# Two-stage kernel of linear attention and a noisy top-2 mixture of experts: key decay ahead of the routing work, weight loads and splits in other steps, a third buffer for x rows, row gathers one by one

## The chip, the cores and the metric

The kernel runs on one core of a Trainium2 chip. The metric is device time in microseconds (us), the median of three runs. Engines are called PE (TensorE matmul), PEld (its weight loads), DVE (VectorE), ACT (ScalarE), POOL (GpSimd) and SP (SyncE, which here only issues DMAs). An engine carries out its instructions in the order of the program, and so does each of the two queues that issue DMAs: SP's (plain copies) and POOL's (gathers and scatters by row index).

## The reference, cut to what matters

Linear attention with decay, over 4 batches, 8 heads, 768 positions and 64 channels, in blocks:

```
intra = (qb @ kb^T * Dmask) @ vb
inter = (qb * lam_pow) @ kv_state
out   = intra + inter
kv_state = lam_block * kv_state + (kb * rev_pow)^T @ vb
```

Its output, seen as x of 3072 tokens by 512 channels, goes into a mixture of 8 experts:

```
noisy = x @ w_gate + log1p(exp(x @ w_noise)) * noise
top2, weights = two largest of noisy, softmax over the two
out[token] += weight * (relu(x[token] @ w1[e]) @ w2[e])     # for both experts e of the token
```

`kb * rev_pow` is what this text calls the **key decay**, and `(kb * rev_pow)^T @ vb` the **state products**.

## The kernel before, in words

**Attention.** The 3072 tokens are 24 chunks of 128; a unit u is two chunks, so there are 12 units. A loop over steps t = 0 to 11 (L885) prepares unit u = t + 1 and finishes unit t. A step issues, in this order: the transposes of the keys (`trans_k`, L297) and of the queries (`trans_q`, L310); the loads of k, q and v of unit t + 3 on SP's queue (L161, L157); the state products (`kv`, L385) and the state update on DVE (`state`, L394 to L398); a portion of routing work (`advance(FILLS)`, L896); the second half of the attention of unit t (`intra`, `inter`, L350) and its copy to SBUF (`evac_o`); the transposes back to token rows (`store_x`, L413: each of a unit's two chunks goes by ACT into a tile `xc`, L414 and L415, and by SP's queue to the rows `x_tok` in DRAM, L417); the gate's products (`products`, L404); the scores of the next unit (`scores`, L338, masked on DVE at L341); and the gate logits (`logits`, L429).

Only then comes `kdecay(t + 2)` (L919): two POOL multiplications (L326) that write the decayed keys of unit t + 2 into the tile `kd`. There is one buffer of `kd`, so they wait for the state products of unit t + 1, and the state products of unit t + 2, in the next step, wait for them. The load of k of unit t + 4 takes the buffer of the keys that `kdecay(t + 2)` reads.

Behind `kdecay` stand, in the same step: the first two row gathers of expert 0, once, in the first step after its lists are there (L920); a weight split, in the steps that the table `SPLITS` names (L927; ACT makes the high part at L747, DVE the low part at L748); a second portion of routing work, `advance(FILL - SPLIT)` in a step with a split and `advance(FILL)` in one without; and a load of 512 KB of weights on SP's queue, in the steps that `LOADS` names (L936). The weights are staged in four `wst` buffers; a load waits for the split of the fourth load before it.

**Routing in portions.** The gate of a group of chunks (`gate`, `weights`, `places`, `build`) is a list of Python generators. `advance(n)` issues their instructions until their costs, as the program puts them (0.21 for most), add up to n. The constants are FILLS = 3.4, FILL = 2.0 and SPLIT = 1.2. Most of it runs on DVE; `weights` (L484 to L500) is issued in one go and is a chain of some 24 small POOL instructions, which begins when the two largest logits are found on DVE (`mx`, L468). The routing of group 0 (chunks 0 to 7) enters the list in step 4, that of group 1 in step 8, that of group 2 after the loop.

**Experts.** Expert 0 takes its tokens in three parts of 2, 2 and 3 tiles of 128 rows (`parts(0)`, the loop at L987), so that it can begin while later tokens are still being routed. Each part is a first matmul over eight blocks f of 128 hidden columns (`gemm1`, L801; ACT and DVE evacuate each block at L807 and L811 into `ht`) and a second one tile by tile (`gemm2`, L839). In the second part, at tile 2, `lists_done` (L970) completes the row lists; it gathers tiles 4 to 6 of expert 0, frees the four `wst` buffers with small POOL copies (L978), and gathers tiles 0 to 3 of expert 1. Ahead of the third part the loop gathers tiles 4 to 6 of expert 1 (L988 to L990). Behind the third part's eight blocks the outputs of tiles 0 to 3 of expert 0 are scattered (L1018 to L1020), and those of tiles 4 to 6 behind their own `gemm2`. From block 4 on, the third part also issues the loads of expert 1's first weights (L1015) and the transposes of expert 1's rows (L1017). A gather or a scatter (L770, L823, L858) moves 128 rows of 2 KB.

Experts 1 to 7 (L1106) do the same in two parts each. There a gather stands behind a one-element POOL copy out of the `ht` block just evacuated (L1121), so that one gather follows each block.

The tile `xc` has the two buffers of its pool, of 2 KB per partition each.

Of the kernel before, what the change touches and what calls it, by code (L numbers as in the profile page):

```python
# [31 lines left out]
C = 128  # L32
# [29 lines left out]
OPUS = 0.21  # L62
FILL, SPLIT, FILLS = 2.0, 1.2, 3.4
FILL1, FILLG = 0.9, 4.6
LOADS = {0: (1, 0), 1: (1, 1), 2: (1, 2), 3: (1, 3), 4: (2, 0), 5: (2, 1), 9: (2, 2), 10: (2, 3)}
SPLITS = {2: (1, 0), 3: (1, 1), 4: (1, 2), 5: (1, 3), 6: (2, 0), 7: (2, 1)}
X1 = ((), (0,), (1,), (2,), (3,), (4,), (5, 6))
WARM = (14, 4, 4)
GB = (0, 8, 16, NCH)
# [52 lines left out]
def kernel(  # L122
# [143 lines left out]
    def advance(n):  # L266
        while n > 0 and jobs:
            j = next(jobs[0], "end")
            if j == "end":
                jobs.pop(0)  # L270
            elif j == "step":
                break
            else:
                n -= j or OPUS
# [114 lines left out]
    def state(u):  # L389

        for a, p in enumerate(KV[u]):
            sn = SA[u + a, 1 - a] = next(states)
            if (u, a) not in SA:
                nc.vector.tensor_copy(sn, p[:, :, :D])  # L394
                continue
            for hp in range(HP):
                nc.vector.scalar_tensor_tensor(sn[:, hp, :], SA[u, a][:, hp, :], QS[:, hp, C - 1:C], p[:, hp, :D],
                                               op0=MULT, op1=ADD)  # L398
# [9 lines left out]
    def store_x(u):  # L408

        for a in range(2):  # L410
            p = bank()
            for d in range(DB):
                nc.tensor.transpose(p[:, d, :], XO[u][:, a, d, :], identf)  # L413
            xc = aw.tile([128, DB, C], FT, name="xc")  # L414
            nc.scalar.activation(xc, p, AF.Copy)  # L415
            g = 2 * u + a
            nc.sync.dma_start(x_tok[g * C:(g + 1) * C, :DM], xc.rearrange("p d i -> p (d i)"))  # L417
# [467 lines left out]
    for t in range(NST):  # L885
        u = t + 1
        if u < NST:
            trans_k(u)
        load(t + 3, "kt")
        if u < NST:  # L890
            trans_q(u)
        load(t + 3, "qt")
        if u < NST:
            kv(u)
            state(u)
            advance(FILLS)  # L896
        else:
            store_x(t - 1)
            products(t - 1)
            for j in range(PARTS0[0]):  # L900
                trans_rows(0, j)
            logits(t - 1)
            advance(FILLS)
        intra(t)
        load(t + 3, "vt")
        inter(t, 0)
        evac_o(t)
        if u < NST:
            if t:
                store_x(t - 1)  # L910
                products(t - 1)
            scores(u)
            inter(u, 1)
            if t:
                logits(t - 1)
        if 2 * t in GB[1:]:
            b = GB.index(2 * t) - 1
            jobs.extend((routing(b), build(early(b))))
        kdecay(t + 2)  # L919
        if REC and not got:  # L920
            for j in range(PARTS0[0]):
                gather_rows(0, j, GB[1] * C)
            got.append(t)
        if built and u < NST:
            enlist(built, False)
            built.clear()
        if t in SPLITS:  # L927
            split_w(SPLITS[t][0], 0, SPLITS[t][1])
        advance(FILL - (SPLIT if t in SPLITS else 0))
        if "w" in RT.get(0, {}):  # L930
            store_w(0)
        if RT.get(0, {}).get("listed") == GM and not REC:
            assert "w" not in RT[0]
            read_lists(0, PARTS0[0])
            load_rec(0)
        if t in LOADS:  # L936
            load_w(LOADS[t][0], 0, LOADS[t][1])
        if t >= NST - 2:
            zero_out(3)
        if t == 2:  # L940
            nc.sync.dma_start(nz, sub(noise, 0, [[E, 128], [128 * E, NCH], [1, E]]))
# [28 lines left out]
    def lists_done():  # L970
        enlist(units[2])
        read_lists(sum(PARTS0[:2]), NTL)
        which_expert(1, nc.sync)
        load_rec(1)
        for j in range(4, 7):
            gather_rows(0, j)
        for _, _, _, buf in units[2]:
            nc.gpsimd.tensor_copy(spacer, buf[0:1, 0:2].bitcast(FT))  # L978
        for j in range(4):
            gather_rows(1, j)  # L980


# [2 lines left out]
        return lambda: [trans_rows(0, t) for t in ts]  # L985

    for i, (t0, n) in enumerate(parts(0)):  # L987
        if i == 2:  # L988
            for t in range(t0, t0 + n):
                gather_rows(1, t)  # L990
        for f in range(FB):
            if i or f >= 2:
                gemm1(0, t0, n, f)
            if i == 0:
                if f == 0:
                    split_w(2, 0, 2)
                elif f < 3:
                    split_w(2, 0, 3, f - 1)
                while f == 3 and len(built) < len(units[1]):
                    advance(0.01)  # L1000
                if 2 <= f < 7:
                    nc.scalar.activation(XG[f], zero, AF.Copy)
                zero_out(2)
                if f == FB - 1:
                    enlist(units[1])
                    read_lists(PARTS0[0], PARTS0[0] + PARTS0[1])
                    for t in range(PARTS0[0], PARTS0[0] + PARTS0[1]):
                        gather_rows(0, t, GB[2] * C)
            if i == 1:
                zero_out(1)  # L1010
                advance(FILL1)
                if "w" in RT[2]:
                    store_w(2)
            if i == 2 and f >= 4:
                load_w(1, 1, f - 4)  # L1015
                for j in X1[f - 4]:
                    trans_rows(1, j)  # L1017
        if i == 2:  # L1018
            for t in range(t0):
                scatter_out(0, t, PV[t])  # L1020
        if i == 0:
            for c in range(0, GB[3] - GB[2], 2):
                units[2].append((2, c, 2, wp.tile([128, F], FT, name="wst", bufs=4).bitcast(BF)))
            advance(FILLG)
        if i == 1:
            finish(2)
            advance(50)
            assert not jobs and "w" not in RT[2]
        then = {1: {12: rows(2, 3)}, 2: {1: lists_done}, 3: {16: rows(4, 5, 6)}}
        for t in range(t0, t0 + n):  # L1030
            gemm2(0, t, then.get(t, {}))
            if t == 0:
                finish(2, "gated")
            if t == 1:
                advance(FILLG)
            if i == 2:
                scatter_out(0, t, PV[t][:size(0, t), :])
            if i == 2:
                for j in range((0, 2, 3)[t - t0], (2, 3, 4)[t - t0]):
                    split_w(1, 1, j)  # L1040
                    load_w(2, 1, j)
                for j in X1[t]:
                    trans_rows(1, j)
# [174 lines left out]
```

## Time and profile before

| | us |
|---|---|
| median of 3 runs | 746.75 |
| the three runs | 745.95, 746.75, 749.08 |
| the profiled execution, its own time | 749.22 |
| its span, first to last instruction | 747.3 |
| PE busy in the span | 722.4 (97%) |
| DVE, ACT, POOL busy | 349.9, 222.6, 237.5 |
| mean granted TensorE clock | 0.988 of full speed |

The profile is one execution; its own time is 1.9 us above its span. The clock column is the share of full speed (2.4 GHz) that the TensorE clock was granted in a stretch: 1.00 is 2.4 GHz and 0.50 is 1.2 GHz. "Idle before" in a timeline row is the time in which that engine did nothing before the row's instruction, with what ended it; "issue" there means that nothing in the profile was waited for. The share of the DMA engines is a mean over 16 of them and can come out a little above 1.

### The profile page before, as it was taken

The numbers are of one execution on the slowest core, as the hardware profiler recorded it, in microseconds if no ns is written. First come the engines' busy times: TensorE is split into PE (matmuls) and PEld (weight loads), VectorE is DVE, ScalarE is ACT, GpSimd is POOL, SyncE is SP. The second block draws the span as 40 slices with busy tenths as digits, with TensorE's granted clock in tenths as the row PEclk, the third lists the DMA queues.
The fourth block names the chain that finished last, engine by engine and source line by source line (L and its number), as shares of the span: only waits on it lengthen the run. The fifth ranks groups of instructions, "written<-read, shape, count | busy, mean of one in ns | idle before, by whom it ended". The sixth has DMA issues, their size and how long they took to land. (4 is left out here: it accounts for less than half of the span.)

```text
span 747.3 us, 15521 instructions
## 1 busy us (share of the span) xinstructions
PE 722.4 (97%) x6170; PEld 618.6 (83%) x6170; DVE 349.9 (47%) x890; ACT 222.6 (30%) x381; POOL 237.5 (32%) x384
## 2 busy tenths in 40 slices
PE   6999989999989999999999999999999999999995
PEld 4888778889878898888888888888888898889884
DVE  5555869769236544443434334434432452335210
ACT  0456544442033321232123212321232242214100
POOL 2311243313613443423441344235222423121311
PEclk9899999999999999999999999999999999999998
DMA  7799955571734634352435153526442543230211
GB/s 183 200 293 239 301 149 168 199 285 30 186 107 143 193 99 156 121 156 58 157 117 155 57 158 116 158 54 178 129 128 72 179 151 104 80 111 25 66 42 38
DMA packets 92052, 103.48 MB, mean 138 GB/s; under 512 B 38582, under 2 KB 64710, under 8 KB 91976
## 3 DMA queue, kind: packets, MB, share of 16 engines
q1 hardware_dynamic: 80408, 66.08, 31.4%
q0 software_dynamic: 11568, 36.37, 15.3%
q8 instruction: 50, 0.82, 0.4%
q14 instruction: 26, 0.21, 0.1%
HBM read 77.93 MB, written 25.74 MB: 139 GB/s over the span
## 5 line engine op out<-in xcount | busy, mean ns | idle before, releaser
L801 PE MATMUL pS<-xth,w1h 128*128 128x512 f32 (+3 forms) x544 | 182.4, 335 | 2.0 <-issue 1.2
L801 PE MATMUL pS<-xth,w1l 128*128 128x512 f32 (+3 forms) x544 | 181.1, 333 | 0.8 <-issue 0.7
L801 PE MATMUL pS<-xtl,w1h 128*128 128x512 f32 (+3 forms) x544 | 181.1, 333 | 0.4 <-issue 0.4
L811 DVE SCALAR_TENSOR_TENSOR ht<-pS,ht 128x256 fp32r<-128x256 f32 (+3 forms) x176 | 76.4, 455 | 136.0 <-ACT ht L807 127.3
L839 PE MATMUL pO<-w2h,ht 128*128 128x512 f32 x384 | 124.4, 395 | 0.0
L839 PE MATMUL pKV<-w2h,ht 128*128 128x512 f32 x384 | 124.3, 394 | 0.0
L807 ACT ACTIVATE ht<-pS 128x512 fp32r<-128x512 f32 (+3 forms) x136 | 65.5, 484 | 188.3 <-PE pS L801 175.2
L858 POOL DMA_INDIRECT out_dram<-ot,rec x46 | 60.0, 1305 | 172.6 <-DVE ot L851 161.9
L801 PEld LDWEIGHTS pS<-xth,w1h 128*128 128x128 f32 x544 | 103.3, 190 | 11.0 <-issue 1.3
L801 PEld LDWEIGHTS pS<-xth,w1l 128*128 128x128 f32 x544 | 103.3, 190 | 10.1 <-issue 1.3
L801 PEld LDWEIGHTS pS<-xtl,w1h 128*128 128x128 f32 x544 | 103.4, 190 | 9.8 <-issue 1.1
L782 ACT ACTIVATE xth<-pS 128x512 fp32r<-128x512 f32 (+2 forms) x53 | 29.8, 573 | 196.7 <-PE pS L780 186.6
L839 PEld LDWEIGHTS pO<-w2h,ht 128*128 128x128 f32 x384 | 72.1, 188 | 14.8
L839 PEld LDWEIGHTS pKV<-w2h,ht 128*128 128x128 f32 x384 | 72.1, 188 | 14.7
L839 PE MATMUL pO<-w2l,ht 128*128 128x512 f32 x192 | 74.9, 390 | 0.0
L839 PE MATMUL pKV<-w2l,ht 128*128 128x512 f32 x192 | 74.9, 390 | 0.0
L770 POOL DMA_INDIRECT xg<-x_tok,rec x46 | 49.8, 1083 | 30.5 <-issue 25.5
L823 POOL DMA_INDIRECT pv<-out_dram,rec x46 | 47.2, 1026 | 29.1 <-issue 26.0
L851 DVE SCALAR_TENSOR_TENSOR ot<-pO,wr,pv 128x512 f32<-128x512 f32 x21 | 15.8, 751 | 79.1 <-PE pO L839 79.1
L851 DVE SCALAR_TENSOR_TENSOR ot<-pKV,wr,pv 128x512 f32<-128x512 f32 x21 | 15.8, 751 | 77.6 <-PE pKV L839 77.6
L326 POOL TENSOR_TENSOR kd<-kt,Mk 128x512 f32<-128x512 f32 x24 | 24.9, 1056 | 72.0 <-PE pR L385 36.2
L748 DVE TENSOR_TENSOR w2l<-wst,w2h 128x1024 fp32r<-128x1024 f32 (+1 forms) x33 | 39.2, 1191 | 11.3 <-ACT w2h L747 11.3
(220 smaller groups left out, 956.9 us busy)
## 6 DMA issues: line engine op xcount, KB each, us to landing
wst<-in_moe_w_dram SPq DMA_DIRECT2D x48, 512.0 KB
wst<-in_moe_w_dram SPq DMA_DIRECT2D x32, 256.0 KB
kt<-in_k_dram SPq DMA_DIRECT2D x12, 512.0 KB
qt<-in_q_dram SPq DMA_DIRECT2D x24, 256.0 KB
vt<-in_v_dram SPq DMA_DIRECT2D x12, 512.0 KB
x_tok<-xc SPq DMA_DIRECT2D x24, 256.0 KB
out_dram<-zero SPq DMA_DIRECT2D x24, 256.0 KB
xg<-x_tok,rec POOLq DMA_INDIRECT x46
```

The lines of the kernel that those rows point to most:

```text
L326: nc.gpsimd.tensor_mul(kd[:, :, s], kt[:, :, s], mask(s, slice(0, HP), slice(C - 1, C)).to_broadcast([128, HP, 2, D]))
L748: nc.vector.tensor_tensor(lo[:, r], st[:, r], hi[:, r].bitcast(FT), op=SUB)
L770: nc.gpsimd.indirect_dma_start(out=XG[t][:size(e, t)], out_offset=None, in_=x_tok[:rows, :], in_offset=bass.IndirectOffsetOnAxis(ap=REC[e, ...
L782: nc.scalar.activation(hi, p, AF.Copy)
L801: nc.tensor.matmul(p, W1[a][d][:, fs], xt(b, cs)[:, d], start=(d == 0 and i == 0), stop=(d == DB - 1 and i == 2))
L807: nc.scalar.activation(ht(e, 0, f, cs), p, AF.Relu)
L811: nc.vector.scalar_tensor_tensor(ht(e, 1, f, c), p[:, r], 0.0, ht(e, 0, f, c).bitcast(FT), op0=OP.max, op1=SUB)
L823: nc.gpsimd.indirect_dma_start(out=PV[t][:size(e, t), :], out_offset=None, in_=out, in_offset=bass.IndirectOffsetOnAxis(ap=REC[e, t], axis=0),
L839: nc.tensor.matmul(p, ht(e, a, f, cs), W2[b][f // 2][:, f % 2, :], start=(i == 0), stop=(i == len(terms) - 1))
L851: nc.vector.scalar_tensor_tensor(o, p, w, pv, op0=MULT, op1=ADD)
L858: st = nc.gpsimd.indirect_dma_start(out=out, out_offset=bass.IndirectOffsetOnAxis(ap=REC[e, t], axis=0), in_=o, in_offset=None, bounds_che ...
```

## The change

Five edits. (1) `kdecay(t + 2)` and the one-time gathers of expert 0 are issued right behind `state(u)`, ahead of the portion of routing work, for steps 0 to 10. (2) The loads of weights move from steps 0, 1, 2, 3, 4, 5, 9, 10 to 0, 1, 4, 5, 7, 8, 9, 10 and their splits from 2 to 7 to 2, 3, 6, 7, 9, 10; with the splits, the larger second portion of routing work moves to steps 4 and 5 and the smaller one to steps 9 and 10. (3) `xc` has three buffers. (4) `lists_done` gathers tiles 0 and 1 of expert 1 instead of 0 to 3; in the third part of expert 0, behind each block f, a one-element POOL copy reads the block and then, for f = 0 to 4, tile f + 2 of expert 1 is gathered. (5) For f = 5 to 7 tile f - 5 of expert 0 is scattered instead; tile 3 follows behind the blocks.

```diff
-LOADS = {0: (1, 0), 1: (1, 1), 2: (1, 2), 3: (1, 3), 4: (2, 0), 5: (2, 1), 9: (2, 2), 10: (2, 3)}
-SPLITS = {2: (1, 0), 3: (1, 1), 4: (1, 2), 5: (1, 3), 6: (2, 0), 7: (2, 1)}
+LOADS = {0: (1, 0), 1: (1, 1), 4: (1, 2), 5: (1, 3), 7: (2, 0), 8: (2, 1), 9: (2, 2), 10: (2, 3)}
+SPLITS = {2: (1, 0), 3: (1, 1), 6: (1, 2), 7: (1, 3), 9: (2, 0), 10: (2, 1)}
...
-            xc = aw.tile([128, DB, C], FT, name="xc")
+            xc = aw.tile([128, DB, C], FT, name="xc", bufs=3)
...
             kv(u)
             state(u)
+            kdecay(t + 2)
+            if REC and not got:
+                for j in range(PARTS0[0]):
+                    gather_rows(0, j, GB[1] * C)
+                got.append(t)
             advance(FILLS)
...
-        kdecay(t + 2)
-        if REC and not got:
-            for j in range(PARTS0[0]):
-                gather_rows(0, j, GB[1] * C)
-            got.append(t)
...
-        for j in range(4):
+        for j in range(2):
             gather_rows(1, j)
...
-        if i == 2:
-            for t in range(t0, t0 + n):
-                gather_rows(1, t)
         for f in range(FB):
             if i or f >= 2:
                 gemm1(0, t0, n, f)
+            if i == 2:
+                nc.gpsimd.tensor_copy(spacer, ht(0, 0, f, columns(0, t0, n))[0:1, 0:1].bitcast(FT))
+                if f < 5:
+                    gather_rows(1, f + 2)
+                else:
+                    scatter_out(0, f - 5, PV[f - 5])
...
         if i == 2:
-            for t in range(t0):
+            for t in range(FB - 5, t0):
                 scatter_out(0, t, PV[t])
```

## Rows read from the trace of the kernel before

**Rows 1.** The page's head and its part 1, the whole span.
```profile
span 747.3 us, 15521 instructions
PE 722.4 (97%) x6170; PEld 618.6 (83%) x6170; DVE 349.9 (47%) x890; ACT 222.6 (30%) x381; POOL 237.5 (32%) x384
```

**Rows 2.** Waits of PE: engine, line, releaser, total us, times, longest us.
```profile
PE pS L385 <- POOL kd L326: 4.8, 4, 2.0
PE pS L338 <- issue: 2.7, 3, 1.6
PE pS L801 <- issue: 2.3, 4, 0.9
```

**Rows 3.** Windows: length, busy of PE, PEld, DVE, ACT, POOL, PEclk, DMA share, GB/s.
```profile
50.79:60.78 9.99, 9.99 (x258) 8.90 (x258) 6.29 (x16) 6.20 (x11) 2.06 (x2) 1.00 0.83 212
60.78:72.04 11.26, 10.41 (x235) 9.08 (x234) 6.26 (x13) 6.25 (x11) 2.06 (x2) 1.00 1.08 292
72.04:82.31 10.27, 10.13 (x259) 8.95 (x258) 8.37 (x31) 6.03 (x11) 2.06 (x2) 1.00 1.01 287
82.31:94.48 12.17, 11.22 (x273) 9.36 (x273) 11.39 (x51) 6.25 (x11) 3.50 (x16) 1.00 1.00 297
94.48:108.81 14.33, 12.18 (x242) 10.72 (x239) 8.93 (x28) 6.03 (x11) 8.41 (x14) 0.88 0.59 159
...
119.38:130.27 10.89, 10.49 (x261) 9.15 (x257) 9.91 (x43) 5.25 (x10) 4.34 (x4) 1.00 0.29 86
130.27:141.16 10.89, 10.89 (x249) 9.27 (x249) 7.94 (x39) 5.15 (x10) 4.83 (x21) 1.00 0.34 122
...
200.07:220.34 20.27, 17.85 (x110) 16.67 (x108) 5.98 (x19) 4.20 (x10) 7.37 (x12) 0.92 0.58 174
...
240.00:738.00 498.00, 498.00 (x2559) 423.61 (x2558) 194.48 (x362) 130.12 (x207) 162.80 (x231) 1.00 0.39 115
```

**Rows 4.** Timeline of PE, steps 6 and 7: start, us, instruction, idle before.
```profile
92.57 0.56 PE L338 MATMUL pS<-qT,kT 64*64 64x128 f32 x12 [0.95 <-issue]
...
98.33 0.33 PE L385 MATMUL pS<-vt,kd 64*64 64x64 f32 x2 [1.47 <-POOL kd L326]
...
99.34 0.86 PE L385 MATMUL pS<-vt,kd 64*64 64x64 f32 x22 [0.68 <-POOL kd L326]
```

**Rows 5.** Timeline of POOL, steps 6 and 7.
```profile
89.71 0.20 POOL L492 TENSOR_TENSOR wa<-mx 128x8 f32<-128x8 f32 x1 [11.95 <-DVE mx L468]
...
97.23 2.06 POOL L326 TENSOR_TENSOR kd<-kt,Mk 128x512 f32<-128x512 f32 x2
```

**Rows 6.** A window of step 7, columns as in rows 3.
```profile
102.00:104.00 2.00, 2.00 (x39) 1.71 (x33) 1.93 (x10) 0.00 (x0) 1.36 (x4) 0.50 1.24 307
```

**Rows 7.** Timeline of ACT, step 4.
```profile
69.46 0.60 ACT L415 ACTIVATE xc<-pS 128x512 f32<-128x512 f32 x1 [0.87 <-DMA x_tok<-xc]
```

**Rows 8.** Groups by line, 20 to 170 us: busy us, mean ns, idle before.
```profile
L748 DVE TENSOR_TENSOR w1l<-wst,w1h 128x1024 fp32r<-128x1024 f32 x4 | 4.9, 1214 | 0.0
```

**Rows 9.** Timeline of DVE, step 10.
```profile
139.08 2.48 DVE L341 TENSOR_TENSOR at<-pS,Mk 128x512 f32<-128x512 f32 x4 [2.88 <-PE pS L338]
```

**Rows 10.** Timeline of POOL, 189 to 228 us: first, last and next of the burst.
```profile
189.61 1.11 POOL L770 DMA_INDIRECT xg<-x_tok,recs  x1 [8.17 <-DVE recs L611]
...
208.12 0.98 POOL L858 DMA_INDIRECT out_dram<-pv,recs  x1 [0.47 <-issue]
...
227.14 1.71 POOL L858 DMA_INDIRECT out_dram<-pv,recs  x1 [17.95 <-DVE pv L854]
```

**Rows 11.** Timeline of SP's queue: expert 1's first weights.
```profile
193.51 4.43 SPq L733 DMA_DIRECT2D wst<-in_moe_w_dram  x6
```

**Rows 12.** Timeline of PE in the third part of expert 0: first and last of four.
```profile
207.76 0.39 PE L801 MATMUL pS<-xth,w1l 128*128 128x320 f32 x1 [0.74 <-issue]
...
210.61 0.62 PE L801 MATMUL pS<-xth,w1h 128*128 128x320 f32 x1 [0.86 <-issue]
```

**Rows 13.** Timeline of ACT in the same part, the first block's evacuation.
```profile
206.37 0.44 ACT L807 ACTIVATE ht<-pS 128x320 fp32r<-128x320 f32 x1 [7.60 <-PE pS L801]
```

## The prediction, made before the changed kernel ran

> **What bounds the kernel now.** I read the page's head first: PE is busy for 722.4 of 747.3 us, no other engine for half of the span [rows 1]. The kernel is a chain of PE work, and what a change can win is PE's idle time, about 25 us, and stretches in which PE works at less than full clock. So the second view is PE's list of waits [rows 2]: three entries are large, 4.8 us for the key decay on POOL, and 2.7 and 2.3 us called "issue", where nothing visible was waited for. The third view is windows cut at the step boundaries (each begins with a step's first key transposes) and at the stages of expert 0 [rows 3]. An undisturbed step takes 9.99 us, without a gap. Step 4 (60.78 to 72.04) takes 11.26, step 6 (82.31) 12.17, step 7 (94.48) 14.33. The third part of expert 0 (200.07 to 220.34) has PE idle for 20.27 - 17.85 = 2.42 us at a mean clock of 0.92. From 240 to 738 PE is never idle: nothing to win there, and a microsecond won earlier reaches the end whole. Only those four places bear on this change.
>
> **Key decay.** In step 7 PE waits 1.47 and 0.68 us for the decayed keys [rows 4], 2.15 together, which is all its idle time there (14.33 - 12.18) [rows 3]. POOL's own timeline tells why [rows 5]: the routing weights' chain was issued in step 6's first portion, ahead of `kdecay(8)`. It waited 11.95 us for DVE, began at 89.71, and the decay could start only at 97.23. Moved ahead of that portion, `kdecay(8)` needs only step 6's state products and takes 2.06 us, a step ahead of its reader; the 2.15 us go. The rest of the 4.8 us lies in the prologue and stays. Behind the gap PE's clock fell to its lower level, 1.2 GHz (0.50 at 102 to 104) [rows 6], with step 7's mean at 0.88 [rows 3]: 0.12 x 14.33 = 1.72 us lost. Without the gap I take that too: **3.87 us**, bounds 2.15 (clock falls anyway) and 4.34 (the step's whole excess over 9.99). What is queued behind on POOL: the weights' chain now follows a 2.06 us decay, but waited for DVE anyway; its reader, a reciprocal in step 7, comes a step later. SP's k load of unit 10, which waited for this decay, goes sooner, so the empty DMA time of step 7 (share 0.59) fills. In the other steps POOL had nothing ahead of the decay, and the move is worth nothing. Expert 0's first gathers stand in step 9, whose first portion holds no POOL work: nothing either.
>
> **The third x buffer.** In step 4 ACT waits 0.87 us for the store that still reads an `xc` tile [rows 7]; PE, short of a PSUM bank, loses 11.26 - 10.41 = 0.85 us, and the step's excess is 1.27. With three buffers a step's first tile reuses one whose store is two steps old, and its second the previous step's first. Steps 2 and 3 also lose a load of 512 KB each, and step 4 runs at a DMA share of 1.08, so the stores land earlier. **1.2 us**, bounds 0 (the queue is late anyway) and 1.27.
>
> **Splits and loads.** A split is 1.21 us on DVE [rows 8]. The program pays for it with 1.2 less of routing work, so a step's DVE load hardly changes where a split leaves or enters; what moves is the routing. By the constants, steps 4 and 5 hold 2.0 instead of 0.8 of second portion: group 0's gate ends at step 5, and step 6's first portion shrinks from 2.84 to 0.42 before the weights' chain breaks it off. That relieves DVE where it was fullest, 11.39 of 12.17 us [rows 3]. Of the step's 2.18 us excess, 0.95 is one gap called issue [rows 4], not DVE's; the rest is late score masks and the counting matmuls. I take **0.5 us**, bounds 0 and 2.18. Against it: the two splits enter steps 9 and 10, where DVE is busy 9.91 and 7.94 of 10.89 us [rows 3]. Group 1's gate then runs 1.2 later, its tail by 1.05 into step 11. In step 10 DVE idles 2.88 us for PE's scores [rows 9], which covers this. **0**, at worst -2.4 (both splits on the path). The loads moved into steps 7 and 8 wait for splits that lie five steps back, so SP's queue isn't held; what stands behind them there are loads for units two steps away. 0.
>
> **Gathers of expert 1.** Between 189.61 and 208.12 POOL issues fourteen transfers, about one per 1.4 us [rows 10], while SP starts 2 MB of weights at 193.51 [rows 11]. PE, in the midst of an accumulation that waits for nobody, then has four gaps up to 210.61 [rows 12], and ACT picks up the first block's evacuation only at 206.37 [rows 13], although its matmuls had started at 200.07. All three engines lag together as POOL issues. After the change five gathers remain ahead of the part; then one transfer follows each block, every (20.27 - 4.0)/8 = 2.0 us, and paces itself: if ACT is late, so is the next gather. Experts 1 to 7 issue theirs in just this way, and PE is never idle in their 498 us [rows 3]. The price of the stretch is 2.42 us idle and 0.08 x 20.27 = 1.62 us of clock, 4.04 in all. I take **3.6 us**, since the weights and the five gathers still meet ahead of 203 us; bounds 0 and 4.9 (with the smeared matmuls around the gaps). POOL was idle from 209 to 227.14 [rows 10], so its new waits for ACT hold up nothing; the last gather goes out at block 4, well ahead of its transposes, which follow the last tile's second matmul, and the scatters' readers come after 240.
>
> What PE lacks in a gap called issue the trace doesn't say. By the Trainium skill's page "Runtime: NRT & Kernel Launch", section "Instruction fetch mechanics", each engine streams its program by DMA in 16 KiB blocks, and the cost of crossing into a block is mostly hidden. If that held here, a full DMA system wouldn't starve PE and spreading the gathers would win nothing; by the rule the sum is 5.6, by the rows 9.2.
>
> **Sum.** 3.87 + 1.2 + 0.5 + 0 + 3.6 = 9.2 us. The profiled execution took 749.22 us (span and 1.9 around it) and would take 740.0. The median of the runs is 2.5 us lower. If that difference lies outside these waits, the median falls to 746.75 - 9.2 = 737.6; if it lies in them, to 740.0. I take **739.0**.
>
> **Rivals.** *The burst is not the cause* (chance 0.20). The gaps at 207 us come from elsewhere, or the same transfers, only later, bring them back. For it: step 6's gap fell at a DMA share of 1.00, with POOL's gathers nowhere near [rows 3, 4], and steps 4 and 5 ran at 1.01 to 1.08 without one. Then 746.75 - 5.6 = 741.2. The skill's rule just named leads here as well.
>
> *Only the gathers pay* (0.10). The time won in steps 4 to 7 is taken by the next thing late: DVE, 8.93 to 11.39 us busy a step, or a DMA system that steps 7 and 8 now keep full. Then 746.75 - 3.6 - 1 = 742.2.
>
> *The change doesn't do what it says* (0.09). The routing portions are counted in costs that aren't times. If the weights' chain were issued in step 5 instead, POOL would again hold it ahead of `kdecay(8)`; and the gathers, though spread, may pile up behind the first five. Both together leave 1 to 2 us: 745.5, no change.
>
> *Slower: issue gaps move into fuller stretches* (0.06). Two loads of 512 KB enter steps 7 and 8, and the formerly empty DMA time of step 7 fills. If a full DMA system is what starves PE, gaps of the kind at 207 (4.0 us with the clock) fall there. The stretch at 207 keeps its own, and only 5.6 is won. From the second such gap on the change loses: two give 746.75 - 5.6 + 8.0 = 749.2, with a third 753. Against it: steps 3 to 5 ran at 0.83 to 1.08 with no issue gap [rows 3].
>
> **How the numbers follow.** The forecast has 0.55, with its own range 735 to 742.5. A measurement of this kernel can tell about 0.5%, 3.7 us, from no change, so faster means below 743.0. Faster: 0.54 of the forecast, 0.16 of the first rival, 0.08 of the second, 0.78. Same: 0.01 + 0.04 + 0.02 + 0.08 + 0.01 = 0.16. Slower: 0.05 of the last and 0.01 of the one before it, 0.06. The range, 735 to 744.5, takes in the bounds of the first four terms downwards (4.34 + 1.27 + 2.18 + 4.0 = 11.8) and the first two rivals upwards; outside it stand the last two.
>
> **What would show it.** Right: no wait of `kv` for `kd` after 20 us; step 7 near 10.3 us with the clock at 1.00; no ACT wait for `x_tok` stores; the third part of expert 0 in about 16 to 17 us, gathers two microseconds apart. Wrong: that stretch again at 20 us, or issue gaps in steps 7 and 8, or step 10 and the head of expert 0 waiting for DVE.

## The result, and the profile after

The changed kernel took **739.11 us** (median of six runs, 737.61 to 741.58). The kernel before took 748.69 beside it (six runs, 745.95 to 754.8): a ratio of **0.9858, 95% interval 0.9809 to 0.9908**. Three later comparisons found the kernel before at 751 to 753 us, so the 746.75 from which the prediction started was a low draw of three.

The page's head, and PE's list of waits, of the changed kernel (engine, line, releaser, total us, times, longest us):

```profile
span 738.0 us, 15537 instructions
PE 719.3 (97%) x6170; PEld 617.2 (84%) x6170; DVE 351.0 (48%) x890; ACT 222.7 (30%) x381; POOL 238.6 (32%) x392
```

```profile
PE pS L338 <- issue: 2.2, 2, 2.0
PE pS L385 <- DVE at L341: 1.9, 1, 1.9
...
PE pS L385 <- POOL kd L326: 0.4, 1, 0.4
```

The span is 9.3 us shorter than in [rows 1]. Against [rows 2], the wait for the key decay fell from 4.8 to 0.4 us, and the issue gaps at L801 are gone. Only the 2.15 us of step 7 were won of that wait: in the prologue most of it now stands under DVE at L341 (1.9 us). What stayed is an issue gap at L338. The windows by step tell more. They begin where those of [rows 3] do: steps 0 and 1, then 4, then 6 to 10, then the third part of expert 0.

```profile
18.77:32.11 13.34, 11.30 (x239) 10.56 (x237) 8.19 (x21) 4.06 (x7) 4.81 (x10) 0.76 0.70 180
32.11:43.08 10.97, 10.81 (x233) 9.48 (x233) 4.54 (x11) 5.10 (x10) 2.06 (x2) 0.96 1.02 274
...
63.19:73.17 9.98, 9.98 (x235) 8.89 (x234) 5.67 (x12) 5.09 (x10) 2.06 (x2) 1.00 0.98 282
...
83.69:94.59 10.90, 10.90 (x272) 9.27 (x273) 8.70 (x43) 6.24 (x11) 5.47 (x17) 1.00 0.82 229
94.59:104.76 10.17, 10.17 (x242) 9.08 (x239) 9.22 (x27) 6.04 (x11) 6.29 (x12) 1.00 0.74 207
104.76:115.69 10.93, 10.78 (x273) 9.45 (x270) 10.17 (x28) 5.09 (x10) 2.06 (x2) 1.00 1.00 266
115.69:126.58 10.89, 10.48 (x261) 9.14 (x257) 9.71 (x42) 6.19 (x11) 4.34 (x4) 1.00 0.37 119
126.58:137.47 10.89, 10.89 (x248) 9.26 (x249) 9.18 (x40) 6.09 (x11) 4.71 (x21) 1.00 0.35 124
195.51:210.81 15.30, 15.30 (x110) 15.28 (x108) 6.17 (x19) 4.42 (x10) 7.55 (x15) 1.00 0.59 166
```

Lay these lengths beside those of before:

| stretch | before | after | difference |
|---|---|---|---|
| prologue, to the first step | 19.39 | 18.77 | -0.62 |
| steps 0 and 1 | 21.27 | 24.31 | +3.04 |
| step 4 | 11.26 | 9.98 | -1.28 |
| step 6 | 12.17 | 10.90 | -1.27 |
| step 7 | 14.33 | 10.17 | -4.16 |
| steps 2, 3, 5, 8, 9, 10 | 62.74 | 63.34 | +0.60 |
| expert 0 up to its third part | 58.91 | 58.04 | -0.87 |
| third part of expert 0 | 20.27 | 15.30 | -4.97 |

The four places that the prediction named won 11.68 us (1.28 + 1.27 + 4.16 + 4.97). Steps 0 and 1 gave 3.04 back, the rest changed by less than one. The kernel before has an issue gap in step 0 too, of 1.60 us (11.27 - 9.67); here it is 2.04 us, and behind it the clock was at 1.2 GHz from 29.55 to 32.97 us, which it wasn't before and which cost 1.7 us. The low mean of step 0, 0.76, comes also from its head, which ran at 1.2 GHz up to 22.73 us, as it did up to 22.52 before. The gap:

```profile
28.83 2.27 PE L338 MATMUL pS<-qT,kT 64*64 64x128 f32 x49 [2.04 <-issue]
```

Now the mechanism, on POOL. The decay of step 6 starts as its state products end, and the routing weights' chain, which stood ahead of it in [rows 5], follows it:

```profile
87.86 2.06 POOL L326 TENSOR_TENSOR kd<-kt,Mk 128x512 f32<-128x512 f32 x2 [8.96 <-PE pR L385]
89.88 0.31 POOL L492 TENSOR_TENSOR wa<-mx 128x8 f32<-128x8 f32 x1
...
98.14 2.06 POOL L326 TENSOR_TENSOR kd<-kt,Mk 128x512 f32<-128x512 f32 x2 [0.99 <-PE pS L385]
```

In the third part of expert 0 the gathers go out every 1.8 us, each behind its block, and ACT takes up a block every 1.76 us, the first 1.95 us into the part (197.46 - 195.51), where it had come after 6.30 us (206.37 - 200.07) [rows 13]:

```profile
198.82 1.03 POOL L770 DMA_INDIRECT xg<-x_tok,rec  x1 [0.61 <-issue]
...
200.58 1.03 POOL L770 DMA_INDIRECT xg<-x_tok,rec  x1 [0.55 <-issue]
```

```profile
197.46 0.44 ACT L807 ACTIVATE ht<-pS 128x320 fp32r<-128x320 f32 x1 [3.26 <-PE pS L801]
199.22 0.44 ACT L807 ACTIVATE ht<-pS 128x320 fp32r<-128x320 f32 x1 [1.32 <-PE pS L801]
```

### The profile page after: what moved, and what is told of

Read it like the earlier page. It is cut to its first block, busy times and chain, and to the rows that moved or that the text cites. A ratio compares the mean times of both kernels' runs of the same rounds, so it can differ in the third digit from the quotient of the medians.

```text
span 738.0 us, 15537 instructions
## 1 busy us (share of the span) xinstructions
PE 719.3 (97%) x6170; PEld 617.2 (84%) x6170; DVE 351.0 (48%) x890; ACT 222.7 (30%) x381; POOL 238.6 (32%) x392
## 5 line engine op out<-in xcount | busy, mean ns | idle before, releaser
L801 PE MATMUL pS<-xth,w1h 128*128 128x512 f32 (+3 forms) x544 | 181.6, 334 | 0.8 <-DVE ht L811 0.8
L801 PE MATMUL pS<-xtl,w1h 128*128 128x512 f32 (+3 forms) x544 | 180.4, 332 | 0.0
L801 PE MATMUL pS<-xth,w1l 128*128 128x512 f32 (+3 forms) x544 | 180.4, 332 | 0.0
L801 PEld LDWEIGHTS pS<-xth,w1h 128*128 128x128 f32 x544 | 102.7, 189 | 9.9 <-DVE ht L811 1.0
L801 PEld LDWEIGHTS pS<-xth,w1l 128*128 128x128 f32 x544 | 102.7, 189 | 8.8
L801 PEld LDWEIGHTS pS<-xtl,w1h 128*128 128x128 f32 x544 | 102.8, 189 | 8.6
```

The source lines that it names most:

```text
L801: nc.tensor.matmul(p, W1[a][d][:, fs], xt(b, cs)[:, d], start=(d == 0 and i == 0), stop=(d == DB - 1 and i == 2))
```

## The experiments

### One edit at a time, on the kernel before

Four kernels ran on one chip, where the kernel before took 752.75 us (27 runs).

**Edit 1 alone, the early decay.**

```diff
             state(u)
+            kdecay(t + 2)
...
-        kdecay(t + 2)
```

> The kernel before with edit 1 alone: the key decay and expert 0's first gathers right behind the state update; loads, splits, x buffers and expert 1's gathers as before. Theory (the decay's place is what cost step 7): the wait of the state products for the decay in step 7 is gone, the clock stays at 1.00, step 7 falls from 14.33 to about 10.3 us, step 6 stays near 12.2, step 4 at 11.3, the third part of expert 0 near 20; total about 4 us below the kernel before. Rival (step 7's excess comes from a full DVE and a full DMA system, the decay only carries the blame): step 7 stays above 12 us. Step 0, which none of these edits should change, tells whether its gap of 1.6 us before and 2.04 us after varies by itself.

Measured: 748.19 us, ratio 0.9938 (0.9915 to 0.9961). Step 7 takes 10.18 us, and `kd` is gone from the list of waits. The third part keeps its gaps (20.77 us), the first of these two rows, and the wait for a free `xc` grew from 0.8 to 2.3 us, the second:

```profile
PE pS L801 <- issue: 2.7, 6, 1.0
...
PE pS L338 <- ACT xc L415: 2.3, 3, 1.4
```

Edit 1 suffices to clear step 7.

**Edits 4 and 5 alone, the spread gathers and scatters.**

```diff
-        for j in range(4):
+        for j in range(2):
             gather_rows(1, j)
...
+                if f < 5:
+                    gather_rows(1, f + 2)
+                else:
+                    scatter_out(0, f - 5, PV[f - 5])
```

> The kernel before with edits 4 and 5 alone: expert 1's gathers and expert 0's scatters one by one behind the blocks. Theory (the burst of fourteen transfers starves the engines): the third part of expert 0 falls from 20.27 to 15.3 us as in the changed kernel, without an issue gap and with its clock at 1.00; total about 5 us below. Rival (the gap falls there by chance, or it needed the attention stage as it was): the part stays near 20 us, or varies; total within 1 us of the kernel before. Attention steps as before.

Measured: 748.73 us, ratio 0.9939 (0.9901 to 0.9977). The third part runs without a gap, and the waits for `kd` stay (4.4 us in all, step 7 at 13.95):

```profile
200.08:215.39 15.31, 15.31 (x110) 15.28 (x108) 6.17 (x19) 4.42 (x10) 6.72 (x13) 1.00 0.63 168
```

The third part's stall needs POOL's transfers in a row: spreading them is worth 4.96 us of the profile with the steps before left as they were.

**Edit 2 alone, weight loads and splits in later steps.**

```diff
-SPLITS = {2: (1, 0), 3: (1, 1), 4: (1, 2), 5: (1, 3), 6: (2, 0), 7: (2, 1)}
+SPLITS = {2: (1, 0), 3: (1, 1), 6: (1, 2), 7: (1, 3), 9: (2, 0), 10: (2, 1)}
```

(`LOADS` likewise.)

> The kernel before with edit 2 alone: other steps for weight loads and splits, and with them other portions of routing work; the decay stands where it stood. Theory (the decay's place is needed): the wait in step 7 stays, step 7 near 14 us, step 6 about 1.3 us shorter (10.9) by the lighter DVE; total 1 to 2 us below. Rival (routing now begins a portion earlier, so the chain on POOL starts at the head of step 6, some 7 us earlier, and the decay behind it is in time even in its old place): no wait in step 7, step 7 near 10.2; total about 5 us below, and edits 1 and 2 each do the same thing.

Measured: 745.93 us, ratio 0.9915 (0.9885 to 0.9945), the largest gain of the four, though the intervals overlap. Its windows: step 6, step 7, the third part.

```profile
84.61:95.01 10.40, 10.40 (x275) 9.31 (x274) 7.90 (x42) 6.19 (x11) 6.73 (x23) 1.00 0.90 249
95.01:105.18 10.17, 10.17 (x242) 9.08 (x239) 9.16 (x28) 6.03 (x11) 3.78 (x6) 1.00 0.80 218
195.90:216.34 20.44, 17.73 (x110) 16.93 (x108) 5.99 (x19) 4.20 (x10) 7.31 (x12) 0.92 0.51 163
```

Step 7 is clean, though the decay still stands at the end of the step. POOL's timeline says why:

```profile
86.00 0.20 POOL L492 TENSOR_TENSOR wa<-mx 128x8 f32<-128x8 f32 x1 [7.40 <-DVE mx L468]
...
92.44 2.06 POOL L326 TENSOR_TENSOR kd<-kt,Mk 128x512 f32<-128x512 f32 x2
```

With the larger portions of routing in steps 4 and 5, DVE has the largest logits 1.39 us into step 6 (86.00 against a step start of 84.61), where it had been 7.40 (89.71 - 82.31) [rows 3, 5]. POOL's chain is over when the decay is due, and the decay ends at 94.50, ahead of step 7. Edits 1 and 2 are two cures of one wait.

**Edit 3 alone, the third x buffer.**

```diff
-            xc = aw.tile([128, DB, C], FT, name="xc")
+            xc = aw.tile([128, DB, C], FT, name="xc", bufs=3)
```

> The kernel before with edit 3 alone: a third buffer for x rows. Theory (the buffer removes step 4's wait): no wait of ACT for stores of x rows, step 4 at 10.0 us instead of 11.26; total about 1.3 us below. Rival (the lighter loads of steps 2 and 3 did it in the changed kernel): step 4 keeps most of its 1.27 us here, and loses it in the run with the loads alone.

Measured: 751.65 us, ratio 0.9996 (0.9966 to 1.0026): nothing. ACT waits longer than before for the stores, and PE behind it:

```profile
ACT xc L415 <- DMA x_tok<-xc: 6.0, 3, 2.2
```

```profile
PE pS L338 <- ACT xc L415: 3.8, 3, 1.7
```

With three buffers a step's second tile still needs the store of the previous step's first. Over all profiles the pattern is plain: ACT waits 1.6 to 6.0 us for `x_tok` stores in each of the seven kernels that lack edit 2 or edit 3 (the two below among them). In the seven profiles with both it never waits, save 0.8 us in one. So it seems that the stores must land earlier and that a buffer more must be there; in no profile did either alone end the wait. The changed kernel without edit 3 was not run.

### Is the loss in step 0 the change's?

**The changed kernel again, on another chip.** No edit.

> The changed kernel once more, unaltered, beside the next two on the same chip. Expected: 0.98 to 0.99 of the kernel before. Its profile gives a second look at step 0 (13.34 us in the first, 11.27 before): if step 0's length is chance, it comes out anywhere between 10.5 and 13.5; the third part of expert 0 stays at 15.3 us and step 7 near 10.2.

Measured: 739.57 us, ratio 0.9848 (0.9795 to 0.9901). Steps 0 and 1, then step 7 and the third part:

```profile
18.53:29.11 10.58, 10.58 (x239) 9.93 (x237) 6.88 (x20) 4.06 (x7) 4.35 (x10) 0.75 0.81 207
29.11:39.11 10.00, 10.00 (x234) 8.91 (x233) 4.86 (x11) 5.09 (x10) 2.07 (x2) 1.00 0.82 218
94.70:104.88 10.18, 10.18 (x243) 9.09 (x239) 9.20 (x27) 6.03 (x11) 6.28 (x12) 1.00 0.77 210
195.73:211.03 15.30, 15.30 (x109) 15.28 (x108) 6.17 (x19) 4.41 (x10) 7.56 (x15) 1.00 0.55 155
```

Steps 0 and 1 take 20.58 us here, less than in the kernel before. Over fourteen profiles step 0 ranges from 10.12 to 13.34 us. Step 7 and the third part repeat to 0.02 us in all profiles that have their edits. But steps 2, 3 and 5 of this run are longer (11.23, 11.51 and 12.01 us against 10.12, 9.99 and 10.52), and the total is the same. Steps 0 to 5 take 64.92 us in the first profile and 65.78 in this one, where six undisturbed steps would take 60: the early steps, whose DMA share lies near 1.0, lose some 5 us, in another step each time.

**The gate's small loads out of step 0.** The changed kernel with the eight loads of gate weights issued on ACT's queue in the prologue.

```diff
+                nc.scalar.dma_start(wgn[h * 64:(h + 1) * 64, d::2, s * E:(s + 1) * E],
...
-                nc.sync.dma_start(wgn[h * 64:(h + 1) * 64, d::2, s * E:(s + 1) * E],
```

> The changed kernel with the eight small loads of the gate's weights (rows of 32 bytes) issued on ACT's queue in the prologue instead of SP's queue in step 0. SP then issues the loads of unit 3 some 6 us earlier, in the time in which the DMA engines are nearly idle now (share 0.22 and 0.12 at 26 to 30 us). Theory (step 0's gap of 2 us is PE waiting for something behind the DMA traffic of that moment, and the early steps suffer from a late DMA system): the gap moves or shrinks, steps 0 and 1 together fall from 24.3 to 21 to 22 us, total 2 to 3 us below the changed kernel. Rival (the small loads collide with the first loads of q, k and v, or the gap stays): the first state products begin later, total equal or 1 to 2 us above.

Measured: 740.57 us, ratio 0.9867 (0.982 to 0.9914): no gain on the changed kernel. Steps 0 and 1 took 21.27 us, but began at 21.12 instead of 18.77, since the prologue's state products now waited for their values (line numbers are 5 higher here):

```profile
16.36 0.34 PE L390 MATMUL pS<-vt,kd 64*64 64x64 f32 x2 [3.12 <-DMA vt<-in_v_dram]
```

Step 0's gap is 0.48 us here. As steps 0 and 1 took 20.58 us in the rerun without this edit, the run doesn't show that these loads make the gap; it shows that moving them ahead only moves a wait.

**What PE lacks in such a gap.** The DMA records of every run have a queue that carries instructions, in packets of 16 KB:

```profile
q8 instruction: 50, 0.82, 0.4%
```

There are 50 of them in each of the fourteen profiles. Behind 240 us one comes for every 210 to 290 matmuls and weight loads of PE, and PE alone has instructions enough for that (2 x 6170), so they are PE's. In the attention loop the fourteen profiles together have 37 issue gaps of over 0.25 us on PE, and 36 of them end 1.25 to 1.59 us after such a packet is through. The gap of step 0 above ends at 28.83; its packet ran from 26.54 to 27.49. So PE seems to wait there for its next instructions. In the 3 us ahead of these 36 gaps the DMA share was 0.75 to 1.18, so a full DMA system probably makes the packet late; no run varied that by itself. Most packets do no harm: some 320 of them came between 18 and 150 us.

### Edits 1 and 2, each beside the other

**The changed kernel without edit 1** (the decay back behind the portion of routing; same chip as the two above).

```diff
-            kdecay(t + 2)
             advance(FILLS)
...
+        kdecay(t + 2)
```

> The changed kernel without edit 1: the decay stands again behind the first portion of routing work and the scores. Theory (edits 1 and 2 do the same thing, as the run with the loads alone suggests, which had no wait for the decay): no wait in step 7, step 7 near 10.2 us, total within 1.5 us of the changed kernel. Rival (each is worth something of its own): step 7 above 11 us, total 2 us or more above the changed kernel.

Measured: 739.44 us, ratio 0.9847 (0.9801 to 0.9893), equal to the changed kernel's 739.57. Steps 6 and 7:

```profile
83.00:93.41 10.41, 10.41 (x275) 9.32 (x274) 8.16 (x42) 6.19 (x11) 6.75 (x23) 1.00 0.98 276
93.41:103.58 10.17, 10.17 (x243) 9.08 (x239) 9.17 (x28) 6.03 (x11) 3.78 (x6) 1.00 0.73 203
```

Beside edit 2, edit 1 wins nothing in step 7, and nothing in the total that these intervals of half a percent could tell.

**The changed kernel without edit 2** (both tables as before, the rest changed; another chip, kernel before 751.45 us).

> The changed kernel without edit 2: weight loads and splits in the steps of the kernel before; the decay, the third buffer and the spread gathers stay. Theory R (edits 1 and 2 are two cures of one wait): no wait for the decayed keys, step 7 at 10.2 to 10.4 us; what edit 2 is worth beside edit 1 is step 6 (11.8 to 12.2 instead of 10.4 to 10.9) and the stores of x rows in steps 2 to 5 (0 to 3 us more): total 740.5 to 744, ratio to the kernel before 0.985 to 0.990. Rival (edit 2 is worth nothing once the decay stands early): step 6 at 10.4 to 10.9, total 739 to 740, ratio 0.984 to 0.985.

Measured: 741.73 us (ten runs), ratio 0.9892 (0.9855 to 0.9929). Steps 6 and 4:

```profile
81.62:92.87 11.25, 11.22 (x272) 9.35 (x273) 10.94 (x50) 6.25 (x11) 4.88 (x15) 1.00 0.91 263
59.78:71.35 11.57, 10.41 (x235) 9.08 (x234) 6.27 (x13) 6.14 (x11) 2.06 (x2) 1.00 1.04 286
```

Step 7 stays clean (10.18), and steps 4 and 6 together take 22.82 us where the changed kernel takes 20.88. That is 1.9 us, with the `x_tok` wait back in step 4 and DVE full again in step 6. The ratio lies on theory R's side, but its interval holds the changed kernel's 0.9848 to 0.9858 too, and this profile's total, 737.63 us, is the shortest of all. Edit 2 beside edit 1 is worth 0 to 3 us; the runs don't settle it closer.

### What stalls the third part

**Plain stores on top.** The changed kernel with sixteen more stores of 256 KB on SP's queue, of zeros, to a DRAM buffer that nobody reads; the computation is complete.

```diff
+                for k in range(2 * f, 2 * f + 2):
+                    nc.sync.dma_start(scr[k * 128:(k + 1) * 128, :], zero[:, :DM])
```

> The changed kernel with sixteen stores of 256 KB more, of zeros to a scratch tensor, issued on SP's queue in the third part of expert 0; the outputs are not touched. The gathers stay one by one. Theory A (a full DMA system, whoever fills it, stalls PE and ACT there): the DMA share is near 1.0 from about 193 to 208 us, issue gaps come back, the part takes 18 us or more instead of 15.3. Theory B (it is POOL's transfers, back to back, that stall them): the DMA share is as high, but there is no gap and the part stays at 15.3 to 15.8 us.

Measured: 741.18 us (one run). The window 190 to 212 us:

```profile
190.00:212.00 22.00, 21.11 (x137) 19.67 (x137) 8.06 (x25) 5.74 (x12) 8.28 (x14) 1.00 1.03 337
```

The DMA engines are full for 22 us (share 1.03), and PE has no issue gap. Its 0.89 us of idle time is one wait of 0.85 us for expert 0's gathered rows. The third part takes 15.29 us, and ACT takes up each of its blocks 0.04 us after the block's last matmul. Full DMA engines by themselves don't stall this part, as theory B had it. The run says nothing on late instructions, since no packet of PE's starts in its third part (the nearest at 189.99 and 212.42).

Look again at the kernel before with this in mind, in two windows ahead of and in PE's gaps, and at the queues in the second (queue, packets, MB, share of 16 engines):

```profile
194.00:206.00 12.00, 12.00 (x74) 10.84 (x73) 2.64 (x8) 1.36 (x3) 9.12 (x12) 1.00 0.99 255
206.00:211.00 5.00, 2.58 (x10) 1.45 (x9) 0.56 (x2) 0.75 (x2) 2.48 (x6) 0.93 1.01 339
```

```profile
q0 software_dynamic: 515, 1.67, 99.6%
q1 hardware_dynamic: 11, 0.02, 1.1%
```

For twelve microseconds the share is 0.99, weights (q1) and POOL's row transfers (q0) mixed, and PE never idles. Then the weights are through. For five microseconds POOL's row transfers alone fill the engines, 1.67 MB, and in these PE works for 2.58 of 5.00 us. The kernel with edit 1 alone shows the same between 203 and 208 us (q0 at 98.9%, PE busy 2.60 of 5.00).

But the stall doesn't begin with PE. This is the last matmul of the part's first block:

```profile
201.68 0.31 PE L801 MATMUL pS<-xth,w1l 128*128 128x320 f32 x1
```

By the profile, which models the ends of matmuls, it ends at 201.99, and ACT takes the block up at 206.37 [rows 13], 4.38 us later, where it takes 0.04 us in the changed kernel. So ACT is held up from 202 us on, in the window in which PE is busy throughout: PE fills the next blocks meanwhile (`pS` has four buffers), and its gaps begin when three blocks are finished. Nor are they late instructions: packets of PE's start at 192.52 and 218.63 us, and PE is back at work at 211 without one.

POOL's own rows don't show this backlog: its last scatter ends at 209.10 (208.12 + 0.98) [rows 10], while the queue moves rows at full share until 211. The Trainium skill's page "Perfetto Trace Analysis", section "DMA Instruction — SWDGE (GPSIMD)", says that such a row ends when the descriptors are made, not when the data has moved; the trace agrees.

**The row of fourteen without the weights.** The kernel before, with expert 1's weights loaded behind the scatters.

```diff
-                load_w(1, 1, f - 4)
...
                 scatter_out(0, t, PV[t])
+            for _, _, _, buf in units[2]:
+                nc.gpsimd.tensor_copy(spacer, buf[0:1, 0:2].bitcast(FT))
+            for j in range(4):
+                load_w(1, 1, j)
```

> The kernel before, with POOL's fourteen gathers and scatters in a row left as they are, but without the 2 MB of expert 1's weights among them: their loads and the POOL copies that free their buffers stand behind the four scatters. Theory 1 (POOL's transfers in a row stall the engines by themselves): the third part of expert 0 keeps its issue gaps after 203 us and takes 19 to 21 us. Theory 2 (the transfers must meet the weights' traffic): no gap there, 15.3 us; gaps, if any, only later, when the weights come. Either way the total is no verdict, since the weights arrive later: within 740 to 756 us.

Measured: 750.03 us (one run). The windows ahead of and in the third part, which starts at 205.52:

```profile
196.00:204.00 8.00, 8.00 (x41) 6.26 (x40) 2.25 (x5) 1.20 (x2) 5.61 (x6) 1.00 0.63 167
204.00:213.00 9.00, 7.49 (x50) 7.21 (x50) 2.34 (x7) 1.26 (x3) 6.72 (x12) 1.00 0.53 175
```

Without the weights the fourteen transfers don't fill the engines (0.53 to 0.63), PE has no issue gap, and the third part takes 15.72 us. The idle 1.5 us is one wait for transposed rows, ahead of it. For PE theory 2 holds. ACT is late all the same:

```profile
214.07 1.30 ACT L807 ACTIVATE ht<-pS 128x320 fp32r<-128x320 f32 x3 [2.53 <-PE pS L801]
```

The first of these three blocks was finished at 211.37, 2.70 us before, and the block ahead of it came 1.49 us late. So POOL's transfers in a row hold up ACT by themselves, at little more than half of the DMA share; here that doesn't make PE idle.

**Only the gathers in a row, only the scatters in a row.** Two variants of the changed kernel: one gathers ten tiles in a row as before and scatters one by one; the other gathers one by one and scatters four tiles in a row.

```diff
-        for j in range(2):
+        for j in range(4):
             gather_rows(1, j)
...
+        if i == 2:
+            for t in range(t0, t0 + n):
+                gather_rows(1, t)
```

> The changed kernel with the ten gathers in a row again (from about 187 to 200 us), and the first three scatters one per block as in the changed kernel. Theory 1a (the gathers in a row stall the engines): issue gaps at about 198 to 207 us, third part of expert 0 at 18 to 20 us, total 742 to 745. Theory 1b (it is the scatters in a row; in the kernel before the first block's evacuation was held up from about 203.6, and the first scatter was issued at 203.94): no gap, 15.3 us, total 739 to 740.

```diff
-                else:
-                    scatter_out(0, f - 5, PV[f - 5])
+                if f == 4:
+                    for t in range(t0):
+                        scatter_out(0, t, PV[t])
```

> The changed kernel with its gathers one per block, but the first four scatters in a row behind the gather of block 4. Theory 1b (scatters in a row stall the engines): issue gaps and a late evacuation within about 2 to 7 us of the first scatter, so in blocks 5 to 7 or the matmuls behind them, 2 to 5 us lost, total 741 to 744. Theory 1a (gathers), and also the theory that all fourteen in a row are needed: no gap, 15.3 us, total 739 to 740.

Measured: 738.26 and 739.37 us, one run each. The first has the third part and, ahead of it, the windows of mixed and of lone row traffic:

```profile
196.00:200.00 4.00, 4.00 (x30) 4.00 (x29) 0.61 (x3) 1.08 (x3) 1.67 (x4) 1.00 1.02 236
200.00:202.00 2.00, 2.00 (x15) 2.00 (x15) 1.07 (x5) 0.46 (x2) 0.27 (x2) 1.00 0.93 336
194.10:209.41 15.31, 15.31 (x110) 15.28 (x108) 5.99 (x19) 4.20 (x10) 5.97 (x14) 1.00 0.57 173
```

The second:

```profile
195.19:210.50 15.31, 15.31 (x110) 15.28 (x108) 6.18 (x19) 4.41 (x10) 7.74 (x14) 1.00 0.61 168
208.50:213.50 5.00, 5.00 (x30) 4.50 (x29) 2.65 (x8) 3.61 (x6) 4.21 (x8) 1.00 0.40 161
```

PE idles in neither. In the first, ACT is late again. The first block's last matmul, and ACT's start on it:

```profile
195.71 0.31 PE L801 MATMUL pS<-xth,w1l 128*128 128x320 f32 x1
198.92 1.10 ACT L807 ACTIVATE ht<-pS 128x320 fp32r<-128x320 f32 x3 [6.12 <-PE pS L801]
```

That is 2.90 us (198.92 - 196.02). Then row transfers alone fill the engines for some 2 us, and ACT is on time (0.04 us at 201.34). In the second, ACT is on time throughout; but its scatters start at 208.60, two microseconds before the part ends, so it hardly tests them. In one run each, either half of the spreading (edit 4 or edit 5) is enough to keep PE from idling.

Over the fourteen profiles ACT's delay divides the runs cleanly. In the six in which POOL's transfers run on in a long row into the part (the kernel before, edits 1, 2 and 3 alone, and the runs without the weights and with ten gathers in a row), ACT takes up its latest block 2.7 to 7.0 us after that block's last matmul. In the other eight it is 0.04 us for every block. In all six the delay ends 1.1 to 1.9 us after POOL has issued its last transfer of the row, whether or not the engines are still full of rows. So the delay goes with POOL's issuing in a row, and not with full DMA engines, nor with row transfers that are still moving. PE itself idles in the four of the six that have the weights and all fourteen transfers. What keeps PE's signal from ACT, why PE goes at one matmul per 0.7 us in its gaps, and what the weights add, isn't shown. No run had a longer row without weights, or one with the four scatters replaced by more gathers.

## Why the prediction was right, point by point

The forecast, 739.0 with a ratio of 0.9896 to its 746.75, lies within 0.2 us of the median and inside the interval of the ratio. The sum was 9.2 us, and the two profiled executions differ by 9.43 (749.22 - 739.79). That closeness is partly luck: the terms together were 2.5 us too small, and the early steps of this profile gave 3 us back. The median hit is luck too: 739.0 is 7.75 us below a low draw of the kernel before, and side by side the medians differ by 9.58.

**Key decay (3.87 predicted).** Step 7 fell by 4.16 us, inside the bounds, and the clock there is 1.00 as assumed. The size and the mechanism on POOL are right; that edit 1 alone brings it is wrong. The step that failed is the one on splits: it followed the moved routing to DVE in step 6, and not on to POOL's chain, which begins with DVE's result. That chain starts 6.0 us earlier in its step (7.40 - 1.39) and so leaves the decay free without edit 1.

It also fits the sum of the single edits. Their gains are 0.62, 0.61, 0.85 and 0.04%, together 2.1%, and the whole change brought 1.4 to 1.5%. The difference, 0.6 to 0.7% or about 5 us, is close to the 4.2 us of step 7, which two of the four count; but the intervals, 0.2 to 0.5% on each ratio, are too wide to show it. Step 7 itself, clear in either run, does.

**Third x buffer (1.2).** Step 4 fell by 1.28 and no `x_tok` wait is left. The prediction named both reasons, the buffer and the loads taken out of steps 2 and 3, and put the whole under the first. Alone the buffer is worth nothing (step 4 took 12.06 us with it), while edit 2 alone brought step 4 from 11.26 to 10.52. These are single profiles of steps that vary.

**Splits and loads (0.5 in step 6, 0 elsewhere).** Step 6 fell by 1.27 here and by 1.8 in the rerun (12.17 to 10.39): inside the bounds, undersized. DVE's load there fell from 11.39 to 8.70, as the step said, and PE no longer idles in it. The cover in steps 9 and 10 held: both take 10.89 us as before, the split lies behind the masks, and DVE's idle time ahead of them shrank from 2.88 us [rows 9] to 1.54:

```profile
135.39 2.48 DVE L341 TENSOR_TENSOR at<-pS,Mk 128x512 f32<-128x512 f32 x4 [1.54 <-PE pS L338]
137.79 1.21 DVE L748 TENSOR_TENSOR w2l<-wst,w2h 128x1024 fp32r<-128x1024 f32 x1
```

**Gathers (3.6, bounds 0 and 4.9).** The third part fell by 4.97, a hair above the upper bound, to 15.30 us with PE never idle. The mis-sized step is the choice of 3.6: it left out the matmuls smeared around the gaps and allowed for a meeting of weights and gathers ahead of 203 us, which costs nothing (10.00 of 10.00 us busy between 190 and 200 at a share of 0.95). The lower end of the range also counts only 4.0 for this term, whose own bound is 4.9. The reading that PE, ACT and DVE lag together as POOL issues was right, and the runs add that ACT lags first.

**Instruction fetch.** The Trainium skill's page "Runtime: NRT & Kernel Launch", section "Instruction fetch mechanics", has the cost of crossing into a new block mostly hidden, and the sum by it was 5.6. The spreading won 4.97 us, so that sum was too small. But the rule isn't refuted by it: the step from "fetches are hidden" to "spreading wins nothing" failed, since no packet of PE's instructions falls in the stall. Nor is it true that the trace doesn't say what PE lacks in an issue gap; the DMA records do, for the attention loop. There the traces agree with "mostly" (36 gaps on some 320 packets), and show what the rest costs, up to 2.04 us a gap.

**The rivals.** The burst was the cause, so the first falls; its argument was sound in one thing, that step 6's gap has nothing to do with gathers (it ends at 92.57, 1.40 us after a packet of instructions). Nothing late took the place of what was won in steps 4 to 7, so the second falls, and the change did what it says, so the third does. Of the slower case a little came true: steps 7 and 8 had no issue gap of over 0.15 us here, at shares of 0.74 and 1.00, but two other profiles with the moved loads have one in step 8, of 0.49 and 0.28 us, where it priced 4.0. What the prediction priced nowhere is how much steps 0 to 5 change from profile to profile, 62.5 to 67.3 us over the fourteen, as large as any of its terms.

## What to carry to other kernels

Where two edits free the same engine at the same moment, price them together: follow a moved piece of work through every queue that waits for its result before crediting the next edit. A transfer issued by row index is not done when its instruction is, and a row of such instructions can hold up other engines: put one behind each block of work. A busy PE hides such a delay as long as it has buffers to fill, so look at how long ACT and DVE take to pick up what PE has finished. Where PE has an issue gap, look in the DMA records for a packet of its instructions just ahead. Where a stretch should run free of waits, price its whole excess over its matmuls at their full rate, and not only the idle time that the trace marks.

## What was not expected of the hardware

Where POOL's gathers and scatters went out in a row, ACT took up its latest block of matmuls 2.7 to 7.0 us after the block was finished, in one run with the DMA engines little more than half busy (0.53 to 0.63); where plain stores kept them full for 22 us (1.03), it took 0.04 us. PE was then slow in the midst of an accumulation that waits for nobody, busy for 2.58 of 5.00 us, with no packet of its instructions on record between 193.4 and 218.6 us. And in the attention loop, 36 of 37 issue gaps of PE end 1.25 to 1.59 us after a packet of its instructions.
